# A fused attention and two-layer network kernel: halves of a tile for partial sums, and a fixed start-up order on VectorE

## The chip, the cores and the metric

The kernel runs on one core of one Trainium2 chip. The metric is the device time of one execution in microseconds (us), the median of several runs. The core's engines work side by side, each through its own list of instructions in order: TensorE (PE in the profile, with its weight loads as PEld), VectorE (DVE), ScalarE (ACT), GpSimd (POOL) and SyncE (SP). All large transfers between DRAM and the core's memory (SBUF) are issued by SP. PSUM is the memory into which TensorE writes its sums.

## The reference

Eight batches, eight heads, 576 positions, 64 values per head, 32 memories; 4608 tokens of 512 values.

```python
a = softmax(phi, axis=2)                        # over the 576 positions
k_m, v_m = a^T k, a^T v                         # 32 memories per head
attn = softmax(q k_m^T / 8)                     # over the memories
x = attn v_m                                    # -> [4608, 512]
h = x @ moe_w_in                                # 512 -> 2048
x = (h - tanh(h)) @ moe_w_out                   # 2048 -> 512
h = max(x @ w1, x @ w2, x @ w3)                 # 512 -> 768
out = h @ w_out2                                # 768 -> 512
```

The weights come as 64-bit floats, `q`, `k`, `v` and `phi` as 32-bit floats.

## The kernel before

**Numbers.** Each factor of the large products is split into a high and a low part, and `mm3` (line 115) makes three matmuls of each product: high by high, high by low, low by high. `conv` (line 160) turns a block of 64-bit weights (`raw`, three buffers) into such parts: two steps on ACT (`cvb`, `cva`), three on DVE (`cvb`), one on POOL (`cva`), and for W_out a cast on ACT and a subtraction on POOL (`wo`).

**Attention.** `phi_gen` takes the maximum of `phi` over the positions (DVE, four steps, `mx`), spreads it over the partitions by PE (`ps_mx`), and takes the exponential; `kv_mm` makes the memories (`ps_kv`, then transposed in `ps_t` to `kT`, `vT`). Per half batch, `q_front` transposes `qt` to `qT` on DVE, `q_score` makes the scores (`sc`), and `q_half` transposes them (`s`), subtracts the maximum, takes the exponential (ACT), sums rows and inverts (`st`, DVE), multiplies (POOL), transposes (`aT`, DVE) and splits into `at` (ACT and POOL). `ps_mx`, `ps_kv`, `ps_t`, `sc` and `ps_w` share two PSUM banks in turn.

**The network.** V and W_in are multiplied first: `vw_gen` makes V W_in for one batch and one quarter of W_in (`ps_w`), ACT casts it and DVE subtracts the cast (`vw`, high and low). A step takes one tile of tokens and one block `fc` of 128 features: `emit_h` makes `ps_h` from `vw` and `at` (two banks), `emit_g` makes tanh (ACT, `th`), `h - tanh(h)` (DVE, `th`), its cast (ACT) and remainder (POOL) in `gh`, and `emit_x` adds twelve matmuls, three for each of four banks `ps_x`, over the feature blocks of a tile. `emit_g` runs three steps ahead of `emit_x` and `emit_h` four.

**Order of the steps.** The features come in two phases of eight blocks. In phase 0 the first four tiles, of 288 tokens each (batches 0 and 1), take blocks 0 to 3 one tile after another (steps 0 to 15), and then blocks 4 to 7 (steps 16 to 31). After that come, for each pair of batches, tiles of 320, 512 and 320 tokens with all eight blocks; the 512-wide tile has 256 tokens of either batch. The sums of a tile at its last block go from `ps_x` to `xo` (DVE and ACT copy them in turn) and to DRAM (`xd`, line 627). Before block 4 the first four tiles load their sums back into `xo` (line 613), and at block 7 DVE adds them (line 620) and they are stored again. `xo` has one buffer.

**What sets the order on the engines.** The code is written as generators, stepped by `slot` between the products. A scheduler then sets the order on each engine, after a timeline that it estimates itself. Ties are added by hand: while `background` is set, an instruction called through V, S, T or G stands behind the `mark` of its engine (`behind`, line 64), without a wait. SP issues its transfers in order. The start (lines 662 to 691) writes out the first instructions by hand: W_in (`w0`) is converted beside `kv_mm(0)`, then come `q_gen(0, 0)`, `vw_gen(0, 0, 0)`, five steps of W_out (`wo0`), and `q_gen(0, 1)` beside six more of W_out.

Of the kernel before, what the change touches and what calls it, by code (L numbers as in the profile page):

```python
# [7 lines left out]
F32 = mybir.dt.float32  # L8
# [3 lines left out]
ALU = mybir.AluOpType  # L12
# [10 lines left out]
def kernel(  # L23
# [43 lines left out]
    background = [False]  # L67
    V, S, T, G = (Paced(e) for e in (nc.vector, nc.scalar, nc.tensor, nc.gpsimd))
    DMA = nc.sync
# [62 lines left out]
            tc.add_manual_dep(b, a.name, mybir.DependencyInfo(mybir.DependencyClass.NoSync, mybir.DependencyReason.DATA), reason="side by side")  # L132


    live = [0]

    def fetch(src):
        live[0] += 1
# [9 lines left out]
    def convs(*jobs, ahead=2):  # L148
        raws, k = [], 0
        for src, hi, lo in jobs:  # L150
            if k == len(raws):
                raws.append(fetch(src))
                yield
            while len(raws) < len(jobs) and live[0] < ahead:
                raws.append(fetch(jobs[len(raws)][0]))
            k += 1
            yield
            yield from conv(raws[k - 1], hi, lo)

    def conv(raw, hi, lo=None):  # L160
        a = cv_p.tile([P, 512], U32, tag="cva", bufs=2, name="cva")
        b = cv_p.tile([P, 512], U32, tag="cvb", bufs=2, name="cvb")
        hw, lw = raw[:, :, 1], raw[:, :, 0]
        S.activation(f(b), f(hw), AF.Abs)
        S.activation(a, lw, AF.Copy, scale=2.0 ** -29)
        yield
        V.tensor_scalar(f(b), f(b), TINY, HUGE, ALU.max, ALU.min)
        V.tensor_scalar(b, b, 3, 0x3FFFFFF8, ALU.logical_shift_left, ALU.bitwise_and)
        yield
        V.scalar_tensor_tensor(out=b, in0=hw, scalar=0xC0000000, in1=b, op0=ALU.bitwise_and, op1=ALU.bitwise_or)  # L170
        live[0] -= 1
        yield
        if lo is None:
            G.tensor_add(hi.bitcast(U32), b, a)
            yield
            return
        G.tensor_add(a, b, a)
        x = f(a).rearrange("p (k c) -> p k c", k=hi.shape[1]) if len(hi.shape) == 3 else f(a)
        S.copy(hi, x)
        yield  # L180
        G.tensor_sub(lo, x, f(hi))
        yield
# [134 lines left out]
    def q_half(b, hf):  # L317
        at = at_t[0, b]
        o = slice(hf * NH, (hf + 1) * NH)
        sp = place(b, 1 if hf else 2, [P, 2, NH], "s")  # L320
        s = sp.rearrange("p e (j m) -> p e j m", m=M)
        scs = scs_t[hf]
        for e in range(2):
            freed[e] = V.transpose(out=sp[:, e], in_=scs[e]).ins
        yield
        st = ap.tile([P, 2, JH, 3], F32, tag="st", bufs=2, name="st")
        V.reduce_max(st[:, :, :, 0], s, axis=AX.X)
        V.tensor_tensor(out=s, in0=s, in1=st[:, :, :, 0:1].to_broadcast([P, 2, JH, M]), op=ALU.subtract)
        yield
        S.activation(sp, sp, AF.Exp, scale=0.125)  # L330
        yield
        V.reduce_sum(st[:, :, :, 1], s, axis=AX.X)
        V.tensor_scalar(st[:, :, :, 2], st[:, :, :, 1], 1e-9, None, ALU.add)
        V.reciprocal(st[:, :, :, 2], st[:, :, :, 2])
        yield
        G.tensor_tensor(out=s, in0=s, in1=st[:, :, :, 2:3].to_broadcast([P, 2, JH, M]), op=ALU.mult)
        yield
        aT = place(b, 0 if hf else 3, [P, 2, NH], "aT")
        V.transpose(out=aT, in_=sp)
        yield  # L340
        at_cast.append(S.copy(at[:, 0, :, o], aT).ins)
        G.tensor_sub(at[:, 1, :, o], aT, f(at[:, 0, :, o]))
        yield
        DMA.dma_start(out=at_d[b][:, :, :, o], in_=f(at[:, :, :, o]))
        yield
# [14 lines left out]
    def q_gen(b, hf):  # L360
        if hf == 0:
            yield from q_begin(b)
        yield from q_front(b, hf)
        yield from q_score(b, hf)
        yield from q_half(b, hf)
        if hf:
            yield from q_next(b)
# [42 lines left out]
    def upto(g, word):  # L410
        for w in g:
            yield
            if w == word:
                return
# [4 lines left out]
    def vw_gen(ph, b, fq):  # L419
        while 2 * ph + fq not in wi:  # L420
            bg.need("wi2")
        t = at_p.tile([P, 2, 2, FQ], F32R, tag="vw", bufs=4, name="vw")
        pss = [bank(e, [P, FQ], "ps_w") for e in range(2)]
        small([(pss[e][32 * r:32 * r + 32], vT[b][64 * e:64 * e + 64, r], wi[2 * ph + fq][64 * e:64 * e + 64, r])
               for r in reversed(range(HP)) for e in range(2)])
        yield
        for e in range(2):
            S.copy(t[:, e, 0], pss[e])
            yield
            freed[e] = V.tensor_sub(t[:, e, 1], pss[e], f(t[:, e, 0])).ins  # L430
            yield
        vw_t[ph, b, fq] = t
# [162 lines left out]
    def at_load(b):  # L595
        at = at_t[1, b] = at_p.tile([P, 2, 2, NS], F32R, tag="at", bufs=3, name="at")
        DMA.dma_start(out=f(at), in_=at_d[b])
        yield

    def emit_x(i):  # L600
        ph, (t0, nt, pcs), fc, first, final = steps[i]
        while 8 * ph + fc not in wo_t:
            bg.need("wo")
        wt = wo_t[8 * ph + fc]
        gh = g_t.pop(i)
        if first:
            emit_x.ps = [ps_x.tile([P, NT], F32, tag=f"x{dm}", bufs=1, name=f"ps_x{dm}")[:, :nt] for dm in range(KD)]
        o = slice(t0, t0 + nt)
        add = ph or t0 < NXI and fc >= 4
        if fc == 4 and add or final and not add:  # L610
            emit_x.xo = ga_p.tile([P, KD, NT], F32, tag="xo", bufs=1, name="xo")[:, :, :nt]
            if add:
                DMA.dma_start(out=emit_x.xo, in_=xd[0][:, :, o])
        for dm in range(KD):
            T.mark = mm3(emit_x.ps[dm], (wt[:, 0, dm * P:(dm + 1) * P], wt[:, 1, dm * P:(dm + 1) * P]),
                (gh[:, 0], gh[:, 1]), first, final)
            if final:
                ps, xo = emit_x.ps[dm], emit_x.xo
                if add:
                    V.tensor_add(xo[:, dm], ps, xo[:, dm])  # L620
                else:
                    (S.copy if dm % 2 else V.tensor_copy)(xo[:, dm], ps)
            if dm == 0 and i + LG < len(steps):
                emit_g(i + LG)
            slot()
        if final:
            DMA.dma_start(out=xd[ph][:, :, o], in_=emit_x.xo)
# [16 lines left out]
    def drain(*gens):  # L644
        gens = list(gens)
        while gens:
            for g in list(gens):
                try:
                    next(g)
                except StopIteration:  # L650
                    gens.remove(g)
# [16 lines left out]
    drain(load_q(0, 1))  # L668
    next(w0)
    drain(phi_gen(0))  # L670
    drain(kv_mm(0), w0)
    wo0 = wo_conv(range(4), wo_p)
    next(wo0)
    next(wo0)
    load_phi(1, fetch.last)
    load_kv(1, fetch.last)
    drain(q_gen(0, 0))
    drain(vw_gen(0, 0, 0))
    for _ in range(5):
        next(wo0)  # L680
    S.mark = at_cast[-1]
    background[0] = True
    drain(q_gen(0, 1), part_of(wo0, 6))
    background[0] = False
    bg.add("wo", wo0)
# [312 lines left out]
```

## Time and profile before

| | |
|---|---|
| time, median of 3 runs | 1346.94 us (1345.87 to 1349.36) |
| the profiled execution's own time | 1347.29 us |
| its span in the profile | 1345.4 us |
| mean granted TensorE clock | 0.989 |
| PE busy (matmuls) | 1273.1 us, 95% |
| PEld busy (weight loads) | 1152.7 us, 86% |
| DVE, ACT, POOL busy | 748.3, 508.0, 530.2 us: 56%, 38%, 39% |
| DMA | 264.94 MB, 197 GB/s on average |

The span runs from the first to the last instruction of the profiled execution; its own time is 1.9 us longer. Busy shares are averages over the whole span. In the rows further below, "PE ps_x L57 <- DVE xo L57" reads: PE, about to write `ps_x`, waited for DVE's work on `xo`. All operations that go through the helper carry its line 57, so tiles tell them apart; DMAs carry their own lines.

### The profile page before, as it was taken

What the parts mean: (1) busy time and instruction counts of PE and PEld (TensorE: products, weight loads), DVE (VectorE), ACT (ScalarE), POOL (GpSimd) and SP (SyncE); (2) the same over time, 40 slices, a digit from 0 to 9 for tenths busy, and PEclk for the clock granted to TensorE, in tenths of its full rate; (3) what the DMA queues carried; (4) which work ended last, traced back from release to release, by engine and by line L of the source; (5) the groups of instructions that cost most, each with busy time, mean ns of one, the idle gap of its engine ahead of it and who ended that gap; (6) DMA issues with size and microseconds to landing.
All of it is one profiled execution on the core that took longest, in us unless ns stands there. A gap on an engine that the chain in (4) does not pass through costs nothing.

```text
span 1345.4 us, 22714 instructions
## 1 busy us (share of the span) xinstructions
PE 1273.1 (95%) x8996; PEld 1152.7 (86%) x8996; DVE 748.3 (56%) x1189; ACT 508.0 (38%) x993; POOL 530.2 (39%) x470
## 2 busy tenths in 40 slices
PE   3579789999999999999999999999999999999998
PEld 1467668888799798998989899899899899999996
DVE  3887648766454665757543335545645556457342
ACT  2445235454344454645553322322322323123221
POOL 1646325654344556766663431232311313123110
PEclk9989889999999999999999999999999999999999
DMA  8886678768162545766672158847557376475532
GB/s 203 233 223 187 151 188 219 226 189 235 36 248 66 182 145 202 279 232 221 235 245 97 52 219 343 321 141 287 175 215 283 106 296 243 124 298 188 176 122 47
DMA packets 188394, 264.94 MB, mean 197 GB/s; under 512 B 94976, under 2 KB 160512, under 8 KB 179200
## 3 DMA queue, kind: packets, MB, share of 16 engines
q1 hardware_dynamic: 188000, 259.82, 59.2%
q0 software_dynamic: 288, 3.67, 0.7%
q8 instruction: 71, 1.16, 0.4%
q14 instruction: 35, 0.29, 0.1%
HBM read 199.49 MB, written 63.96 MB: 196 GB/s over the span
## 4 chain that ended last, share of the span: by engine, by line
PE 84%; DVE 6%; SPq 3%; DMA 3%; issue 2%; POOL 1%; ACT 1%; DVEq 0%; POOLq 0%; ACTq 0%
PE b L57 41%; PE ps_x L57 26%; PE ps_h L57 13%; SPq L224 3%; DVE cvb L57 2%; PE ps_w L57 2%; PE ps_kv L57 1%; DMA raw<-in_moe_w_out_dram 1%; DVE th L57 1%; DMA xo<-xd 1%; DVE st L57 1%; DMA phi<-in_phi_dram 1%; ACT cvb L57 1%; DVE s L57 0%; PE sc L57 0%
## 5 line engine op out<-in xcount | busy, mean ns | idle before, releaser
L57 PE MATMUL ps_x<-gh,wo 128*128 128x320 f32 (+2 forms) x2400 | 453.7, 337 | 17.5 <-DVE xo L57 13.7
L57 PEld LDWEIGHTS ps_x<-gh,wo 128*128 128x128 f32 x2400 | 383.2, 192 | 62.3 <-issue 22.9
L57 PE MATMUL b<-mv,sw 128*128 128x384 f32 x2268 | 401.4, 338 | 0.0
L57 PEld LDWEIGHTS b<-mv,sw 128*128 128x128 f32 x2268 | 399.1, 188 | 1.2
L57 POOL TENSOR_TENSOR gh<-th,gh 128x320 fp32r<-128x320 f32 (+2 forms) x200 | 207.5, 1039 | 250.8 <-ACT gh L57 237.6
L57 PE MATMUL ps_h<-at,vw 128*128 128x256 f32 (+2 forms) x1536 | 247.9, 301 | 13.2 <-DVE th L57 6.7
L57 PEld LDWEIGHTS ps_h<-at,vw 128*128 128x128 f32 x1536 | 221.9, 191 | 37.8 <-DVE th L57 12.5
L57 DVE TENSOR_TENSOR th<-ps_h,th 128x320 f32<-128x320 f32 (+2 forms) x200 | 106.9, 535 | 180.0 <-ACT th L57 179.3
L57 ACT ACTIVATE th<-ps_h 128x320 f32<-128x320 f32 (+2 forms) x200 | 95.4, 477 | 176.2 <-PE ps_h L57 162.3
L57 PE MATMUL b<-wz,mh 128*128 128x512 f32 x648 | 150.4, 390 | 1.1 <-DVE ob L57 1.1
L57 PEld LDWEIGHTS b<-wz,mh 128*128 128x128 f32 x648 | 121.3, 188 | 26.4 <-DVE ob L57 2.0
L57 ACT CAST gh<-th 128x320 fp32r<-128x320 f32 (+2 forms) x200 | 99.9, 499 | 108.4 <-DVE th L57 90.9
L57 POOL TENSOR_TENSOR c<-c,u 128x384 f32<-128x384 f32 x36 | 36.5, 1013 | 226.2 <-ACT u L57 226.2
L57 ACT COPY p<-b 128x384 f32<-128x384 f32 x108 | 51.7, 479 | 169.5 <-PE b L57 147.0
L57 DVE TENSOR_TENSOR c<-b,u 128x384 f32<-128x384 f32 x72 | 39.8, 553 | 97.4 <-PE b L57 97.4
L57 DVE TENSOR_SCALAR cvb<-cvb 128x512 f32<-128x512 f32 x112 | 67.3, 601 | 32.3 <-ACT cvb L57 29.9
L57 DVE TENSOR_TENSOR m<-c,m 128x768 f32<-128x768 f32 x72 | 69.0, 958 | 5.0
L57 DVE TENSOR_TENSOR c<-b,p 128x384 f32<-128x384 f32 x72 | 37.7, 554 | 37.9 <-ACT p L57 34.4
L57 DVE TENSOR_TENSOR vw<-ps_w,vw 128x512 fp32r<-128x512 f32 x64 | 41.3, 682 | 28.1 <-ACT vw L57 28.1
L57 POOL TENSOR_TENSOR mv<-xr,mv 128x384 fp32r<-128x384 f32 x30 | 48.9, 1663 | 12.4 <-PE b L57 9.3
L57 POOL TENSOR_TENSOR m<-m,u 128x384 f32<-128x384 f32 x18 | 21.4, 1188 | 81.6 <-ACT u L57 80.2
L57 ACT CAST mh<-m 128x384 fp32r<-128x384 f32 (+1 forms) x54 | 31.8, 620 | 57.1 <-DVE m L57 57.1
(82 smaller groups left out, 1048.5 us busy)
## 6 DMA issues: line engine op xcount, KB each, us to landing
sw<-sw_d SPq DMA_DIRECT2D x52, 1792.0 KB, 7.5
sw_d<-so SPq DMA_DIRECT2D x9, 1792.0 KB, 7.5
raw<-in_moe_w_out_dram SPq DMA_DIRECT2D x22, 512.0 KB, 5.4
qt<-in_q_dram SPq DMA_DIRECT2D x128, 72.0 KB, 3.3
at_d<-at SPq DMA_DIRECT2D x16, 576.0 KB, 5.3
at<-at_d SPq DMA_DIRECT2D x8, 1152.0 KB, 5.7
raw<-in_moe_w_dram SPq DMA_DIRECT2D x18, 512.0 KB, 4.0
out_dram<-ob SPq DMA_DIRECT2D x144, 64.0 KB, 1.7
```

Of the source, the lines that this page charges most:

```text
L57: i = op(*a, **kw)
L224: q_dma.dma_start(out=t[64 * e + 32 * h:64 * e + 32 * h + 32, r], in_=src[e, h, r])
```

## The change

Two things. First, `xo` becomes a pair of halves for the first four tiles: one tile `two`, 576 columns wide, made once, of which tiles 0 and 2 use the left half and 1 and 3 the right (`part_x`). Loads of partial sums into it are written in `emit_x` two steps ahead of a tile's block 4, not in it. Second, the start is written out anew: `V.mark` is set to the second transpose of the scores, then to the last step of the last W_in block, then to the reciprocal of the row sums, then to the last subtraction of V W_in, so that on DVE scores, last W_in block, row sums, V W_in and W_out follow in that order.

```diff
-    live = [0]
+    live, wi_last, st_last = [0], [None], [None]
@@ convs
+            if k == len(jobs):
+                yield "last"
             yield from conv(raws[k - 1], hi, lo)
@@ conv
-        V.scalar_tensor_tensor(out=b, in0=hw, scalar=0xC0000000, ...)
+        wi_last[0] = V.scalar_tensor_tensor(out=b, in0=hw, scalar=0xC0000000, ...).ins
@@ q_half
-        V.reciprocal(st[:, :, :, 2], st[:, :, :, 2])
+        st_last[0] = V.reciprocal(st[:, :, :, 2], st[:, :, :, 2]).ins
@@
+    def part_x(t0):
+        k = t0 // NH % 2
+        return emit_x.two[:, :, k * NH:(k + 1) * NH]
+
@@ emit_x
-        add = ph or t0 < NXI and fc >= 4
-        if fc == 4 and add or final and not add:
-            emit_x.xo = ga_p.tile([P, KD, NT], F32, tag="xo", bufs=1, name="xo")[:, :, :nt]
+        parted = ph == 0 and t0 < NXI
+        add = ph or parted and fc >= 4
+        if i == 0:
+            emit_x.two = ga_p.tile([P, KD, 2 * NH], F32, tag="xo", bufs=1, name="xo")
+        if parted:
+            emit_x.xo = part_x(t0)
+        elif fc == 4 and add or final and not add:
+            emit_x.xo = ga_p.tile([P, KD, 2 * NH], F32, tag="xo", bufs=1, name="xo")[:, :, :nt]
             if add:
                 DMA.dma_start(out=emit_x.xo, in_=xd[0][:, :, o])
+        ph1, (t1, n1, _), fc1, _, _ = steps[min(i + 2, len(steps) - 1)]
+        if ph1 == 0 and t1 < NXI and fc1 == 4:
+            DMA.dma_start(out=part_x(t1), in_=xd[0][:, :, t1:t1 + n1])
@@ the start
-    drain(kv_mm(0), w0)
+    drain(kv_mm(0), upto(w0, "last"))
     wo0 = wo_conv(range(4), wo_p)
     next(wo0)
     next(wo0)
     load_phi(1, fetch.last)
     load_kv(1, fetch.last)
-    drain(q_gen(0, 0))
-    drain(vw_gen(0, 0, 0))
+    drain(q_begin(0), q_front(0, 0))
+    drain(q_score(0, 0))
+    x = q_half(0, 0)
+    next(x)
+    V.mark = freed[1]
+    background[0] = True
+    drain(w0)
+    V.mark = wi_last[0]
+    next(x)
+    next(x)
+    background[0] = False
+    y = vw_gen(0, 0, 0)
+    next(y)
+    next(x)
+    V.mark = st_last[0]
+    background[0] = True
+    drain(x, y)
+    V.mark = freed[1]
     for _ in range(5):
         next(wo0)
     S.mark = at_cast[-1]
-    background[0] = True
     drain(q_gen(0, 1), part_of(wo0, 6))
     background[0] = False
```

The first place is SP's list from the store of tile 2's first sums on. `xd_120` holds the partial sums in DRAM; `phi`, `kv` and `qt` are loads for the next batches. Before:

```order
L627 DMA xd_120<-xo 512x1x288
L198 DMA phi<-in_phi_dram 128x8x128
L199 DMA phi<-in_phi_dram 64x8x32
L211 DMA kv<-in_k_dram 128x8x256
L214 DMA kv<-in_k_dram 64x8x64
L211 DMA kv<-in_v_dram 128x8x256
L214 DMA kv<-in_v_dram 64x8x64
L224 DMA qt<-in_q_dram 32x18x32 x8
L627 DMA xd_120<-xo 512x1x288
L224 DMA qt<-in_q_dram 32x18x32 x7
L613 DMA xo<-xd_120 128x4x288
L224 DMA qt<-in_q_dram 32x18x32
```

After:

```order
L641 DMA xd_120<-xo 512x1x288
L627 DMA xo<-xd_120 128x4x288
L200 DMA phi<-in_phi_dram 128x8x128
L201 DMA phi<-in_phi_dram 64x8x32
L213 DMA kv<-in_k_dram 128x8x256
L216 DMA kv<-in_k_dram 64x8x64
L213 DMA kv<-in_v_dram 128x8x256
L216 DMA kv<-in_v_dram 64x8x64
L226 DMA qt<-in_q_dram 32x18x32 x8
L641 DMA xd_120<-xo 512x1x288
L226 DMA qt<-in_q_dram 32x18x32 x8
L627 DMA xo<-xd_120 128x4x288
```

The load of tile 0's sums moved from behind the second group of `qt` loads to right behind tile 2's store; the load of tile 1's sums (the last row of after) keeps its place behind sixteen `qt` loads.

The second place is DVE's list in the start. `cvb` is a block of weights, and takes two `TENSOR_SCALAR` and one `SCALAR_TENSOR_TENSOR`: in the rows of before the first such block is the last one of W_in, the second the first one of W_out. Before:

```order
L57 TENSOR_SCALAR cvb<-cvb 128x512 x2
L57 SCALAR_TENSOR_TENSOR cvb<-raw,cvb 128x512
L57 STREAM_TRANSPOSE qT<-qt 128x576
L57 TENSOR_SCALAR cvb<-cvb 128x512
L57 STREAM_TRANSPOSE s<-sc 128x288 x2
L57 TENSOR_SCALAR cvb<-cvb 128x512
L57 TENSOR_REDUCE st<-s 128x18
L57 SCALAR_TENSOR_TENSOR cvb<-raw,cvb 128x512
L57 TENSOR_TENSOR s<-s,st 128x576
L57 TENSOR_TENSOR vw<-ps_w,vw 128x512
L57 TENSOR_REDUCE st<-s 128x18
L57 TENSOR_SCALAR st<-st 128x18
```

After:

```order
L57 STREAM_TRANSPOSE s<-sc 128x288 x2
L57 TENSOR_SCALAR cvb<-cvb 128x512 x2
L57 SCALAR_TENSOR_TENSOR cvb<-raw,cvb 128x512
L57 TENSOR_REDUCE st<-s 128x18
L57 TENSOR_TENSOR s<-s,st 128x576
L57 TENSOR_REDUCE st<-s 128x18
L57 TENSOR_SCALAR st<-st 128x18
L57 RECIPROCAL st<-st 128x18
L57 TENSOR_TENSOR vw<-ps_w,vw 128x512
L57 STREAM_TRANSPOSE aT<-s 128x576
L57 TENSOR_TENSOR vw<-ps_w,vw 128x512
L57 TENSOR_SCALAR cvb<-cvb 128x512
```

The last W_in block now stands behind the transposes of the scores and ahead of the maximum, the row sums stand ahead of both subtractions `vw`, and the first W_out block begins behind these.

The third place is the entry of batch 3 (`vT_92` holds its V) at the first 512-wide tile, on PE. `wo_962` to `wo_964` are the W_out parts of the last three blocks of the 320-wide tile before it; the four numbers behind `ps_x` are its four banks, and `ps_x_2756` is a bank of the 512-wide tile. Before:

```order
L57 MATMUL ps_x_2495<-gh,wo_962 128x320 x3
L57 MATMUL ps_x_2496<-gh,wo_962 128x320 x3
L57 MATMUL ps_w<-wi,vT_92 32x512 x8
L57 MATMUL ps_x_2497<-gh,wo_962 128x320 x3
L57 MATMUL ps_x_2498<-gh,wo_962 128x320 x3
L57 MATMUL ps_h<-at,vw 128x256 x6
L57 MATMUL ps_x_2495<-gh,wo_963 128x320 x3
L57 MATMUL ps_x_2496<-gh,wo_963 128x320 x3
L57 MATMUL ps_h<-at,vw 128x256 x2
L57 MATMUL ps_x_2497<-gh,wo_963 128x320 x3
L57 MATMUL ps_x_2498<-gh,wo_963 128x320
L57 MATMUL ps_h<-at,vw 128x256 x3
```

After:

```order
L57 MATMUL ps_x_2491<-gh,wo_964 128x320 x3
L57 MATMUL ps_t<-ident,n 64x128 x4
L57 MATMUL ps_w<-wi,vT_92 32x512 x8
L57 MATMUL ps_h<-at,vw 128x256 x10
L57 MATMUL ps_w<-wi,vT_92 32x512 x8
L57 MATMUL ps_h<-at,vw 128x256 x2
L57 MATMUL sc<-qT,kT 32x288 x8
L57 MATMUL ps_h<-at,vw 128x256 x12
L57 MATMUL ps_x_2756<-gh,wo_296 128x512
```

On DVE, at the same place, after:

```order
L57 TENSOR_TENSOR n<-ps_kv,rc 128x2x2x64
L57 TENSOR_TENSOR mx<-phi 128x256
L57 COPY xo<-ps_x_2488 128x320
L57 TENSOR_TENSOR mx<-mx,phi 128x256
L57 COPY xo<-ps_x_2490 128x320
L57 TENSOR_TENSOR mx<-mx,phi 128x256 x2
L57 TENSOR_TENSOR vw<-ps_w,vw 128x512 x4
L57 TENSOR_TENSOR th<-ps_h,th 128x512
```

V W_in of batch 3 moved on PE from among the products of the old tile to behind the last of them, and on DVE the four `vw` stand behind the four `mx`, which are batch 5's maximum; before, DVE had the four `vw` (two pieces, with `cvb` between) right ahead of the first 512-wide `th`, and the `mx` further ahead.

## Rows read from the trace of the kernel before

**Rows 1.** Windows: busy us of each engine (instructions), granted clock, DMA share, GB/s.

```profile
core 0: us, PE busy (x) PEld busy (x) DVE busy (x) ACT busy (x) POOL busy (x), PEclk, DMA share, GB/s
0.00:1345.40 1345.40, 1273.13 (x8996) 1152.72 (x8996) 748.26 (x1189) 507.97 (x993) 530.18 (x470) 0.99 0.60 197
145.00:150.00 5.00, 0.64 (x16) 0.10 (x16) 0.00 (x0) 1.30 (x2) 0.00 (x0) 1.00 0.79 123
185.00:190.00 5.00, 0.43 (x2) 0.43 (x3) 0.94 (x3) 0.00 (x0) 0.00 (x0) 0.50 0.82 175
200.00:250.00 50.00, 50.00 (x512) 42.20 (x511) 39.49 (x67) 26.91 (x50) 27.94 (x25) 1.00 0.72 196
```

**Rows 2.** Waits from 100 to 215 us: us in total, times, longest us.

```profile
DVE xo L57 <- DMA xo<-xd: 15.4, 3, 7.2
PE ps_x L57 <- DVE xo L57: 13.7, 2, 7.0
```

**Rows 3.** Timeline of SP: start us, us, operation, count.

```profile
114.34 0.52 SPq L627 DMA_DIRECT2D xd<-xo  x1
...
131.02 10.27 SPq L224 DMA_DIRECT2D qt<-in_q_dram  x8
141.39 0.57 SPq L627 DMA_DIRECT2D xd<-xo  x1
142.06 5.09 SPq L224 DMA_DIRECT2D qt<-in_q_dram  x7
147.20 0.63 SPq L613 DMA_DIRECT2D xo<-xd  x1
...
184.69 0.58 SPq L613 DMA_DIRECT2D xo<-xd  x1
```

**Rows 4.** Timeline of PE around its two waits for `xo`.

```profile
138.92 1.75 PE L57 MATMUL ps_x<-gh,wo 128*128 128x288 f32 x12
...
152.66 6.17 PE L57 MATMUL ps_x<-gh,wo 128*128 128x288 f32 x28 [7.01 <-DVE xo L57]
...
162.54 2.92 PE L57 MATMUL ps_x<-gh,wo 128*128 128x288 f32 x20
...
189.57 8.87 PE L57 MATMUL ps_x<-gh,wo 128*128 128x288 f32 x46 [6.70 <-DVE xo L57]
```

**Rows 5.** Timeline of the start, by engine.

```profile
41.97 1.26 POOL L57 TENSOR_TENSOR wo<-cva,wo 128x512 fp32r<-128x512 f32 x1 [0.73 <-ACT wo L57]
...
42.06 1.20 DVE L57 TENSOR_SCALAR st<-st 128x18 f32<-128x18 f32 x1
...
47.88 2.77 PE L57 MATMUL ps_h<-at,vw 128*128 128x288 f32 x10 [0.64 <-POOL at L57]
...
69.13 1.43 DVE L57 STREAM_TRANSPOSE qT<-qt 128x576 f32<-128x576 f32 x2
...
87.65 0.18 DVE L57 TENSOR_SCALAR st<-st 128x18 f32<-128x18 f32 x1
```

**Rows 6.** Waits of DVE from 28 to 50 us.

```profile
DVE cvb L57 <- ACT cvb L57: 3.7, 3, 2.2
DVE aT L57 <- POOL s L57: 0.7, 1, 0.7
DVE vw L57 <- ACT vw L57: 0.6, 1, 0.6
```

**Rows 7.** DMA issues from 120 to 155 us: KB each, median us to landing.

```profile
phi<-in_phi_dram SPq DMA_DIRECT2D x1, 512.0 KB, 4.4
```

**Rows 8.** Timeline from 206 to 229 us, around batch 3's first V W_in.

```profile
206.47 0.84 SPq L198 DMA_DIRECT2D phi<-in_phi_dram  x1
...
213.41 0.42 DVE L57 TENSOR_TENSOR mx<-phi 128x256 f32<-128x256 f32 x1 [1.23 <-DMA phi<-in_phi_dram]
...
213.93 3.11 DVE L57 TENSOR_TENSOR mx<-mx,phi 128x256 f32<-128x256 f32 x3
...
216.97 1.09 PE L57 MATMUL ps_w<-wi,vT 64*32 64x512 f32 x16
...
220.10 1.06 ACT L57 CAST vw<-ps_w 128x512 fp32r<-128x512 f32 x2
...
220.71 1.29 DVE L57 TENSOR_TENSOR vw<-ps_w,vw 128x512 fp32r<-128x512 f32 x2 [1.01 <-ACT vw L57]
```

More of the change, by code (lines that the diff above doesn't have):

```diff
@@ L169, in conv @@
         yield
-        V.scalar_tensor_tensor(out=b, in0=hw, scalar=0xC0000000, in1=b, op0=ALU.bitwise_and, op1=ALU.bitwise_or)
+        wi_last[0] = V.scalar_tensor_tensor(out=b, in0=hw, scalar=0xC0000000, in1=b, op0=ALU.bitwise_and, op1=ALU.bitwise_or).ins
         live[0] -= 1
```

## The prediction

> **What bounds the kernel now.** I read the stretches first, then TensorE's waits, then the queue that serves the longest wait. TensorE (PE) is busy for 1273.1 of 1345.4 us, so only its idle time and its slow time can be won. In 200 to 250 us it is busy throughout; ahead of that, two stretches stand out: PE does 0.64 of 5 us in 145 to 150 and 0.43 of 5 us in 185 to 190, where the granted clock is 0.50, the lower of its two levels (1.2 instead of 2.4 GHz) [rows 1]. One wait makes both: PE wants a `ps_x` bank, and VectorE (DVE) has not emptied it, 13.7 us in two waits; DVE itself stands before the same additions for 15.4 us in three, because `xo` has not been loaded [rows 2].
>
> The queue says why [rows 3]. The sums of the first four tiles' first half wait in DRAM and come back through one tile `xo`. The store of tile 2 left at 114.34, and no load could go until tile 3's sums had been copied into the same `xo` and stored. That store (141.39) stands behind eight `qt` loads (131.02, 10.27 us), the first load behind seven more (142.06, 5.09 us). It left at 147.20; the twelve products whose sums it was for had ended at 140.67 [rows 4]. Tile 2's load has the same fate: it waits for tile 1's sums to be loaded, added and stored behind another batch's loads, and left at 184.69. DVE runs in order, so while it waits nothing else of its work goes on either: 0.00 us busy in 145 to 150 [rows 1].
>
> **The change, part by part.** *The two halves.* Tiles 0 and 2 use one half, 1 and 3 the other, and a load is written two steps ahead. In the new order tile 0's load stands right behind tile 2's store, that is at about 115 instead of 147, some 26 us ahead of its use. Tiles 2 and 3 get their loads right behind the stores of tiles 0 and 1. The number of transfers and of additions stays. So both waits go: **-13.7 us**. With them goes the slow clock behind each: 28 products took 6.17 us and 46 took 8.87, while 20 of the same shape took 2.92 at full clock, 0.146 each [rows 4]. 28 x (0.220 - 0.146) + 46 x (0.193 - 0.146) = **-4.2 us**.
>
> *Tile 1's load* stays behind the sixteen `qt` loads, at about 147.9 on the old clock, and lands some 5 us later (issued at 147.20 [rows 3], the wait over at 152.66 [rows 4], less an addition), so at about 152.7. Without the first wait PE reaches the end of tile 1 early: from 140.7 (the end of tile 0's last step) 48 products of `ps_x`, 24 of `ps_h` and some small ones, 74 x 0.146 = 10.8 us, to 151.5, and then 16 score products and six more `ps_h`, 1.5 us by estimate, before the bank is wanted. That is a tie: **+1 us**, bounds 0 (a quicker landing) and 4 (a landing as late as the second wait is long, less the lead).
>
> *DVE's order up to the first tile.* It removes and adds nothing but order; the same W_out pieces come before the first `th`. DVE's avoidable waits in 28 to 50 are 0.7 for `aT`, 0.6 for `vw`, and 3.7 - 2.2 = 1.5 for `cvb` (the 2.2 is the load of the last W_in block, which stays) [rows 6]. To these comes a stretched instruction: `st` took 1.20 at 42.06 and 0.18 at 87.65 [rows 5], 1.0 us. So at most 3.8 us. What stays on the path: scores, maximum, exponential, sum, GpSimd's product, transpose, `at`, each on the engine before. The ten `ps_h` products that started at 47.88 [rows 5] move ahead by at most that, but the first `ps_x` also needs W_out, which now comes wholly behind V W_in, and GpSimd has four W_out pieces ahead of the first `gh`. I take **-2 us**, the middle of 0 and -4.
>
> The `st` of 1.20 us began while GpSimd was in a W_out piece (41.97, 1.26 us [rows 5]). The Trainium skill, SBUF — State Buffer, section "SBUF: two separate sides", says that VectorE and GpSimd share a port pair as an exclusive lock: whichever starts first keeps it for its whole instruction. By that rule the W_out pieces, now close together, would stretch each other again and the start-up gain would be near 0; the sum would be 2 us higher. The row agrees with it, one time.
>
> *What is late next.* The scheduler places later work anew, and one place tells. Batch 3 enters at the first 512-wide tile. Its V W_in needs PSUM banks that `ps_kv` and `ps_t` of batch 4 hold first. Before, it stood 42 `ps_x` products ahead of that tile's first step; now it stands behind the last product of the tile before, and on DVE its low parts (`vw`) stand behind all four `mx` of batch 5. These wait for a load of `phi` which only the end of batch 4's `ps_kv` lets go. The nearest case of before: `phi` issued at 206.47, the first `mx` at 213.41 after a wait for it, the last one over at 217.04, 10.6 us in all [rows 8]. A quicker landing of `phi` is 4.4 us [rows 7]; with four `mx` of 0.42 and two copies, taken as long, that makes 6.9. PE needs 4.4 us from that issue to the end of the old tile (24 products of 320 columns at 0.146 x 320/288 = 0.162, and a few short ones, 0.5 in all at the 0.07 of a `ps_w` product [rows 8]). So `vw` starts V = 2.5 to 6.2 us after PE has run dry. From there: two subtractions 1.29, the second V W_in product (sixteen matmuls) 1.09, two casts 1.06 [rows 8], the rest of the subtractions 0.65, scores and six `ps_h` 1.5, tanh and cast about 0.6 each = V + 6.8 until `ps_x` can go on, while PE's own work there is `ps_t`, two V W_in, scores and 24 `ps_h`, 6.5 us by estimate. So PE loses V + 0.3 = 2.8 to 6.5, middle 4.7, plus up to 2 us for a lowered clock (the two waits above cost 2.1 each at 7 us idle). I take **+5.5 us**, bounds 0 (the placing does no harm) and 9. The steps' lead gives no cover here, since PE has by then used up its three steps.
>
> *The rest.* From 205 us on PE has few waits, and all DMA and attention work that follows is released by PE or DVE, so it moves ahead with them: 0, bounds -1 and +2. The tile `xo` is 576 instead of 512 columns wide: nothing waits for its size.
>
> Sum: 1347.3 (the profiled execution; its span is 1345.4, the 1.9 around it stays) - 13.7 - 4.2 + 1 - 2 + 5.5 = 1333.9. The profiled execution lies 0.35 above the median of the runs, so **1333.5 us**, 1.0% less.
>
> **The rivals.** *Nothing is handed back:* batch 3's V W_in is ready in time because `phi` lands quickly and PE's lead holds; for it, that PE is busy in all 50 us of 200 to 250 now [rows 1], so leads do hold; against it, the order. 1346.9 - 13.7 - 4.2 - 2 + 0.5 = 1327.5. *More is handed back:* tile 1's load comes 4 us late and the entry of batch 3 costs 9; for it, that the queue is pressed just there: eight `qt` loads took 10.27 us at 131.02, against 5.09 for the seven after [rows 3]. 1346.9 - 17.9 + 4 + 9 - 1 = 1341. *The halves do not part:* if the wait were on the whole tile, load 2 would still wait for tile 1's store and both waits would stay: 1345 with the start-up's gain; in the new order the load stands ahead of that store, which speaks against it. *Slower than before:* the queue at the start. The fourth W_out load waits for a `raw` buffer which DVE frees with the first W_out block, now behind V W_in, and thirteen `qt` loads of batch 1 stand behind it. They take 0.7 each (5.09 for seven [rows 3]), 9 us; their use is at 69.13 and they could leave from about the first `ps_h`, 47.88 [rows 5], which with 5 us of landing leaves some 7 us of slack. Each us beyond it delays batch 1 and all behind it; from some 20 us of waiting on, the 13.4 us are gone and the kernel is slower, 1349 at 23. Nothing in the trace makes a W_out block that late.
>
> **How the numbers follow.** Forecast (part is handed back, 1329 to 1338) 0.60; nothing handed back 0.16; more handed back (1338 to 1344) 0.15; halves don't part 0.04; slower by the queue 0.05. The range reaches from the middle of the second to past the middle of the third: 1327 to 1342. Differences under 0.3%, 4 us, cannot be told from none here: faster by more is the first three cases less the late end of the third, 0.87; same 0.08; slower 0.05.
>
> **What would show it.** Right: no wait of PE on DVE's `xo` over 2 us, full clock in 140 to 185, the first load of `xo` at about 115; PE idle in several pieces of 1 to 2 us ahead of the first 512-wide `ps_x`, with DVE waiting for `phi`. Wrong: a wait of DVE's `xo` on the load of tile 1 over 4 us; the first `ps_h` not earlier than 47; batch 1's `qT` waiting for `qt`; a new wait later than 205 us that gives away more than 9 us.

## The result, and the profile after

The changed kernel is slower: 1353.42 us, median of 7 runs (1350.09 to 1362.58), against 1346.94 for the kernel before (7 runs, 1343.29 to 1349.36). The ratio is 1.0072, with a 95% interval from 1.0049 to 1.0096. I had forecast 1.0% less. The profiled execution took 1350.09 us, with a span of 1348.2; it is the fastest of the seven, and its mean granted clock is the highest, 0.989 against 0.978 to 0.986 in the others.

Windows of the profile after, the columns as in [rows 1]:

```profile
0.00:1348.20 1348.20, 1274.54 (x8996) 1153.32 (x8996) 747.37 (x1189) 506.95 (x993) 534.11 (x470) 0.99 0.60 197
50.00:70.00 20.00, 13.35 (x67) 12.88 (x67) 16.77 (x26) 8.95 (x20) 16.85 (x13) 0.74 0.60 143
145.00:150.00 5.00, 5.00 (x40) 5.00 (x39) 3.51 (x11) 2.16 (x6) 2.39 (x3) 1.00 0.90 202
185.00:190.00 5.00, 5.00 (x35) 5.00 (x36) 4.43 (x8) 2.25 (x5) 2.15 (x3) 1.00 1.00 283
200.00:260.00 60.00, 53.26 (x613) 41.74 (x614) 38.88 (x66) 23.63 (x44) 27.63 (x23) 0.91 0.72 202
240.00:250.00 10.00, 8.21 (x166) 5.81 (x165) 7.50 (x11) 4.48 (x8) 9.29 (x8) 0.62 0.33 114
```

The two holes of [rows 1] are full: PE works through 145 to 150 and 185 to 190 at full clock. A new hole lies in 200 to 260, where PE is idle for 6.7 us and the granted clock falls to 0.62 in 240 to 250; and the start runs at 0.74 in 50 to 70, where the kernel before had 0.91:

```profile
50.00:70.00 20.00, 15.34 (x92) 12.89 (x92) 19.21 (x30) 9.10 (x19) 15.01 (x12) 0.91 0.68 185
```

The waits for `xo` from 100 to 215 us, which were 15.4 and 13.7 in [rows 2]:

```profile
DVE xo L57 <- DMA xo<-xd: 2.5, 1, 2.5
...
PE ps_x L57 <- DVE xo L57: 0.3, 1, 0.3
```

And the queue that fed them, SP's timeline (compare [rows 3]):

```profile
119.09 0.53 SPq L641 DMA_DIRECT2D xd<-xo  x1
122.38 0.59 SPq L627 DMA_DIRECT2D xo<-xd  x1
...
135.01 8.81 SPq L226 DMA_DIRECT2D qt<-in_q_dram  x8
143.93 0.57 SPq L641 DMA_DIRECT2D xd<-xo  x1
144.60 5.80 SPq L226 DMA_DIRECT2D qt<-in_q_dram  x8
150.44 0.63 SPq L627 DMA_DIRECT2D xo<-xd  x1
```

The first load now leaves at 122.38, behind the store of tile 2; tile 1's load, behind the sixteen `qt` loads, costs the one wait that is left.

So the holes are gone, and the time went elsewhere. Where it went is read from the steps: a step ends with its twelfth `ps_x` product, so every twelfth of PE's 2400 such products gives the end of one. The table holds them for the profiled executions, as differences from the kernel before (negative is ahead). The kernels of the experiments stand beside it for later.

| end of step | before, us | changed | halves alone | start alone, no further step | further step alone | halves, V W_in first, W_out late |
|---|---|---|---|---|---|---|
| 0 | 54.69 | +3.57 | +0.32 | -0.22 | -0.09 | +1.24 |
| 19 | 140.66 | +4.23 | -0.19 | +6.80 | -0.78 | +0.69 |
| 32 | 208.36 | -19.66 | -21.28 | +2.67 | -4.62 | -20.82 |
| 39 | 231.03 | -19.58 | -21.21 | +2.39 | -4.83 | -20.88 |
| 40 | 235.48 | -8.43 | -11.13 | +2.39 | -4.84 | -14.66 |
| 43 | 249.41 | +3.22 | -3.98 | +2.39 | -4.84 | -14.41 |
| 48 | 274.49 | +1.02 | -6.22 | +2.39 | -4.00 | -14.00 |
| 103 | 475.41 | -0.34 | -6.18 | +3.60 | -2.54 | -12.26 |
| 152 | 641.29 | +2.49 | -6.18 | +3.60 | +0.28 | -12.26 |
| 199 | 792.62 | +2.49 | -6.18 | +3.60 | +0.27 | -12.26 |

The changed kernel begins some 4 us late, is 19.6 us ahead at step 39, and has lost it all by step 43. Two cautions. The kernel with the further step alone has the order of before on every engine up to 218 us and was still 4.62 us ahead at step 32: two executions of one order differ by that much. And being ahead by steps is not all gain, since small products (`ps_kv`, `ps_w`, `sc`) may have moved behind the step: the last column loses 6.5 us between steps 39 and 43 while PE is hardly idle. So a second table gives PE's idle time (span less busy time) by stretches, from the windows; a slow clock shows in it as longer busy time.

| PE idle, us | before | changed | halves alone | start alone, no further step | further step alone | halves, V W_in first, W_out late |
|---|---|---|---|---|---|---|
| 0 to 140 | 48.9 | 51.7 | 48.3 | 50.7 | 49.5 | 49.0 |
| 140 to 200 | 13.8 | 2.3 | 3.4 | 10.4 | 11.2 | 3.0 |
| 200 to 260 | 0.0 | 6.7 | 5.3 | 0.0 | 0.0 | 0.2 |
| 260 to 400 | 0.9 | 1.8 | 0.4 | 0.0 | 1.6 | 0.6 |
| 400 to the end | 8.7 | 11.2 | 8.6 | 8.6 | 11.0 | 8.7 |
| idle in all | 72.3 | 73.7 | 65.9 | 69.7 | 73.3 | 61.5 |
| busy in all | 1273.1 | 1274.5 | 1273.2 | 1279.4 | 1272.5 | 1271.9 |

Against before, the changed kernel wins 11.5 us of idle time in 140 to 200 and loses 2.8 ahead of it, 7.6 in 200 to 400, and 2.5 behind.

The entry of batch 3, step 40, on PE and DVE (timeline, profile after):

```profile
207.76 3.69 PE L57 MATMUL ps_x<-gh,wo 128*128 128x320 f32 x24
...
211.38 0.66 PE L57 MATMUL ps_t<-ident,n 128*64 128x128 f32 x8
...
211.59 0.43 DVE L57 TENSOR_TENSOR mx<-phi 128x256 f32<-128x256 f32 x1 [1.70 <-DMA phi<-in_phi_dram]
...
212.57 1.09 PE L57 MATMUL ps_w<-wi,vT 64*32 64x512 f32 x16 [0.53 <-ACT vT L57]
...
214.37 1.29 DVE L57 TENSOR_TENSOR vw<-ps_w,vw 128x512 fp32r<-128x512 f32 x2 [0.36 <-ACT vw L57]
...
219.16 0.72 PE L57 MATMUL sc<-qT,kT 64*32 64x288 f32 x16 [1.62 <-DVE vw L57]
...
221.34 0.62 PE L57 MATMUL ps_x<-gh,wo 128*128 128x512 f32 x2
```

Behind it, steps 41 to 43, on SP, ACT and PE:

```profile
217.02 7.62 SPq L226 DMA_DIRECT2D qt<-in_q_dram  x8
...
225.42 5.98 SPq L226 DMA_DIRECT2D qt<-in_q_dram  x8
...
230.93 2.22 PE L57 MATMUL ps_x<-gh,wo 128*128 128x512 f32 x8
...
232.11 3.04 SPq L141 DMA_DIRECT2D raw<-in_moe_w_out_dram  x2
...
237.53 0.66 ACT L57 ACTIVATE cvb<-raw 128x512 f32<-128x512 f32 x1 [6.53 <-DMA raw<-in_moe_w_out_dram]
...
239.35 1.63 POOL L57 TENSOR_TENSOR gh<-th,gh 128x512 fp32r<-128x512 f32 x1 [7.49 <-ACT gh L57]
...
242.14 0.71 PE L57 MATMUL ps_kv<-ones,phi 128*32 128x1 f32 x40 [1.79 <-issue]
...
248.42 4.21 PE L57 MATMUL ps_x<-gh,wo 128*128 128x512 f32 x9
```

The first fence is the forecast term: `ps_x` stands from 211.4 to 221.3 while V W_in is made and split; the load of `phi` (1.70) plays a smaller part in it than the turns between PE, ACT and DVE. The second fence was in no term. ACT stood for 6.53 us before the load of a W_out block, which SP could issue only at 232.11 behind sixteen `qt` loads; casts and tanh were queued behind it (`gh` on POOL waited 7.49), and after the idle pieces nine products took 4.21 us at 248.42, 0.47 each, where eight of that width had taken 2.22 at 230.93, 0.28 each.

### The profile page after: what moved, and what is told of

Read it like the earlier page. It is cut to its first block, busy times and chain, and to the rows that moved or that the text cites. A ratio compares the mean times of both kernels' runs of the same rounds, so it can differ in the third digit from the quotient of the medians.

```text
span 1348.2 us, 22719 instructions
## 1 busy us (share of the span) xinstructions
PE 1274.5 (95%) x8996; PEld 1153.3 (86%) x8996; DVE 747.4 (55%) x1189; ACT 506.9 (38%) x993; POOL 534.1 (40%) x470
## 4 chain that ended last, share of the span: by engine, by line
PE 81%; DVE 6%; DMA 6%; SPq 3%; issue 2%; ACT 2%; POOL 1%; DVEq 0%; ACTq 0%; POOLq 0%
PE b L57 40%; PE ps_x L57 24%; PE ps_h L57 12%; DVE cvb L57 2%; DMA raw<-in_moe_w_out_dram 2%; PE ps_w L57 2%; PE ps_kv L57 2%; SPq L226 2%; DMA phi<-in_phi_dram 1%; DMA kv<-in_v_dram 1%; DMA sw<-sw_d 1%; DVE th L57 1%; DVE st L57 1%; ACT cvb L57 1%; PE sc L57 1%
## 5 line engine op out<-in xcount | busy, mean ns | idle before, releaser
L57 ACT COPY p<-b 128x384 f32<-128x384 f32 x108 | 51.7, 479 | 170.2 <-PE b L57 141.9
L57 POOL TENSOR_TENSOR mv<-xr,mv 128x384 fp32r<-128x384 f32 x30 | 48.9, 1662 | 12.4 <-ACT mv L57 12.4
```

The costliest lines, as they stand in the source:

```text
L57: i = op(*a, **kw)
```

## The experiments

All ratios are against the kernel before on the same chip, whose median lay between 1344.2 and 1346.0 us there. "The further step" is a third part of the change that I found only on the way; it comes with experiment 9. The step times in some of the expectations are off: counted product by product, as in the table, the changed kernel's first step ends 3.6 us late and the sixteenth 4.2, the waits that are gone give 23.8, and steps 40 to 43 take 22.8 back, 11.2 of it at step 40; the halves alone give back 17.2 of 21.2, 10.1 of it at step 40.

**1 and 2: the halves alone, the start alone.** The first is the kernel before with `part_x`, `two` and the early loads (and none of the rest); the second is the changed kernel with `emit_x` of before.

> The two halves alone, with the start as before. In the trace of the changed kernel the first step ends 2.9 us later than before, the sixteenth 4; the two waits for xo then give 21, and steps 40 to 43 (the first 512-wide tile) take 19 of it back. Theory 1, the chain of batches (scores, V W_in and the next batch's memories take turns in two PSUM banks, and this chain did not move when the waits went): the chain starts 4 us earlier than in the changed kernel, so all that follows does: 1346 to 1349, about the time before, and the loss of the changed kernel is its start. Rival, the start costs nothing in the end, since slack behind it takes it up: 1350 to 1354, like the changed kernel.

> The fixed order of VectorE at the start alone, xo as before. Theory 1: the 3 to 4 us of the start stay to the end, since nothing behind it has slack while the two waits for xo remain: 1350 to 1352. Rival, the waits for xo take the late start up (they wait for a queue, not for the start): 1346 to 1348.

Measured: halves 1341.53 us, ratio 0.998 (0.9967 to 0.9994); start 1355.40 us, 1.0087 (1.0068 to 1.0106). Neither number is what theory 1 gave: the halves are 0.2% faster, and the start with all else of the change costs more than the whole loss. The halves alone are at 1341 in microseconds, the time of my second rival, but the kernel before was at 1344.24 beside them; on the forecast's 1346.9 their ratio gives 1344.

**3 and 4: the two places of the hand-back, each cured alone in the changed kernel.** Experiment 3 issues V W_in of batch 3 before the memories of batch 4; experiment 4 begins the second half of W_out later.

```diff
# 3, in q_beside, for b == 3: the memories of the next batch last
+        if b == 3:
+            for g in (x, y, x, y, x, y, x):
+                yield next(g, None)
+            yield from y
+            yield "half"
+            yield from m
+            return
# and ("q", 0, 3) is queued behind ("vw", 0, 3, fq)
# 4
-        bg.add("wos", wo_store(fc), start[0, 2])
+        bg.add("wos", wo_store(fc), start[0, 2] + 24)
```

> The changed kernel, with V W_in of batch 3 issued ahead of the memories of batch 4 and not behind them; nothing else is changed, and the work is the same. In its order both V W_in of batch 3 stand at steps 38 and 39.5 and not behind step 40. Theory 1: step 40 loses its wait, some 9 of the 19 us are kept, 1341 to 1345 by the profiled execution of the changed kernel (1350). Rival 1, the chain is only shifted: batch 4's memories come later by the same, and its first tile (step 56) or the slow clock takes the time back, 1349 to 1354. Rival 2, the loss lies in the W_out conversions at steps 41 to 43 alone: step 40 stays as long, no gain, 1350 to 1354.

> The changed kernel, with the conversion of the second half of W_out begun 24 steps later (step 56 and not 32), so that ScalarE does not wait for its weights (6.5 us in one wait, with tanh and cast queued behind it) in steps 40 to 43. Theory of that wait: the 9.6 us that steps 41 to 43 hand back are kept, 1341 to 1345, and step 40 still loses 9. Theory 1: what ScalarE gains there is not on the chain of batches, and the time comes back by step 56: 1347 to 1353.

Measured: V W_in first 1352.43 us, 1.0068 (1.0046 to 1.0091), no gain on the changed kernel; W_out late 1344.08 us, 0.9997 (0.998 to 1.0013), 0.7% better than it. In experiment 3 rival 1 holds, though not at step 56: it loses 6.2 us at step 40 where the changed kernel loses 11.2, is 9.3 us ahead of before at the end of step 43, and 1.7 at the end of step 64, the first step of the 512-wide tile that batch 5 enters. The wait was moved to the next such tile. Experiment 4 gives 9 us by the medians (5.4 by the profiled executions), and where the wait on ACT was priced: over steps 41 to 43 it loses 4.4 us against before, the changed kernel 11.7.

**5 and 6: one turn less in the chain.** A batch's `ps_kv`, `ps_t`, two `ps_w`, two `sc` and `ps_mx` take turns in the two small banks. Both kernels leave out the maximum of `phi` for batches 2 to 7, in the halves and in the kernel before.

```diff
+        if b >= 2:
+            S.activation(ph, ph, AF.Exp)
+            yield
+            ph_t[b] = ph
+            yield
+            return
         mx = ap.tile([P, H, M], F32, tag="mx", bufs=1, name="mx")
```

> The two halves alone (start as before), and for batches 2 to 7 the maximum of phi is neither taken nor subtracted: that leaves out one of the seven turns that a batch takes in the two small PSUM banks (two products on TensorE of 1.1 us per batch, 6.8 in all, and some 4.5 us per batch on VectorE). In its order V W_in of batch 3 stands at steps 30 and 32 and not at 40. To be read against the same cut in the kernel before. Theory 1, the chain of turns took the gain back: without one turn the gain of the halves stays, 15 to 20 us below the kernel before with the same cut: about 1319. Rival, the gain is lost elsewhere: 2 to 6 us below it, about 1333.

> The kernel before with the same cut as in the run above: no maximum of phi for batches 2 to 7. The two waits for xo stay, as they hang on the queue and not on the chain. TensorE loses 6.8 us of products: 1337 by both theories; if it falls by much more (under 1330), the chain bounded the kernel before as well.

Measured: halves 1333.55 us, 0.9907 (0.9889 to 0.9925); before 1342.18 us, 0.9967 (0.9954 to 0.9981). So with the cut the halves are worth 0.6%, 8.6 us, and without it 0.2%. That is three times as much and half of what theory 1 said. The kernel before gains 3.4 us by the cut, half of the 6.8 of the products left out. One reason is in the waits of the cut kernel before, whose holes are smaller (13.7 in [rows 2]):

```profile
PE ps_x L57 <- DVE xo L57: 8.7, 2, 5.2
```

And of that gain nothing is lost at the entry: the cut halves are 6.1 us ahead of the cut kernel before at the end of step 39 and at that of step 43, and PE has no idle time there, against 5.3 us in the halves without the cut (windows of 200 to 260 us, first with, then without the cut):

```profile
200.00:260.00 60.00, 60.00 (x554) 50.04 (x553) 35.72 (x63) 30.26 (x57) 34.61 (x29) 1.00 0.64 187
```

```profile
200.00:260.00 60.00, 54.73 (x649) 42.57 (x649) 43.13 (x74) 26.40 (x50) 30.55 (x26) 1.00 0.76 211
```

Batch 4's `ps_kv` starts at 167.1 us in the cut halves and at 201.7 in the halves. The cut takes out a turn in the banks and DVE's steps for the maximum at once, so which of the two the chain hung on is not shown.

**7 and 8: which tie of the start, and W_out late in the halves.** Experiment 7 takes from the changed kernel the tie that holds W_out behind V W_in; experiment 8 is experiment 4's edit on the halves.

```diff
# 7
     drain(x, y)
-    V.mark = freed[1]
+    V.mark = None
+    background[0] = False
     for _ in range(5):
         next(wo0)
     S.mark = at_cast[-1]
+    background[0] = True
```

> The changed kernel without one of its four ties: W_out's conversion on VectorE is no longer held behind V W_in (its first block stands among the scores again); scores, last W_in block, row sums and V W_in stay tied. Theory S, holding back W_out is what the start costs (ScalarE then stands 3.1 us before the load of the third W_out block, and the first products of ps_x wait for W_out): 1341 to 1344, like the two halves alone. Rival, the order among scores, W_in and V W_in costs it: 1349 to 1354.

> The two halves alone, with the conversion of the second half of W_out begun at step 56 and not 32. The halves alone gave back 8 of 19 us at steps 40 to 43, 6 at step 40 and 2 behind it. Theory of the wait on ScalarE (5.5 us there too): the 2 behind step 40 are kept, and what the queue is relieved of: 1337 to 1340. Rival, in the changed kernel the late start was what made that wait cost time, here it costs nothing: 1341 to 1343.

Measured: W_out free 1354.12 us, 1.0046 (1.0026 to 1.0067); halves with W_out late 1342.17 us, 0.9968 (0.9953 to 0.9984), no clear gain on the halves. Experiment 7 did not fit theory S, and its steps said why: it was 18.2 us ahead at step 39, and 8.3 behind at step 199. The start could not be what it lost between these. Something of the change acts all along the program.

**9 to 12: the further step.** `convs` now yields "last" before the last block of every call, though only the first W_in conversion has a reader for it. The conversions are paced by counting steps, so each block of W_out's second half takes nine and not eight, and all later work is placed anew.

```diff
# 9 and 11: the halves, and the kernel before, with this alone
             k += 1
             yield
+            if k == len(jobs):
+                yield "last"
             yield from conv(raws[k - 1], hi, lo)
# 10 and 12: the changed kernel, and the start alone, without it elsewhere
-            if k == len(jobs):
+            if tell and k == len(jobs):
                 yield "last"
# tell is set by wi_conv(0) alone
```

> The two halves with the start as before, and one more thing of the change that the runs so far kept apart from neither: convs hands out the word last ahead of the last block of every job, which is one step more for every paced conversion of weights (9 steps and not 8 for each block of the second half of W_out, of w1 to w3's and of w_out2's). Theory Y, this step, and not the start, costs the time, since it puts the conversions at other places all along the program: 1349 to 1354. Rival S, the order of the start costs it: 1340 to 1343, like the halves alone.

> The changed kernel, with the word last handed out for the first W_in conversion alone, where the start needs it; halves and start order as changed. Theory Y: 1340 to 1346 (the halves alone, plus the 2 to 4 us by which the first steps end later). Rival S: 1350 to 1354, as changed.

> The kernel before with nothing but the further step in every conversion. Theory Y: slower, 1350 to 1356, with the two waits of 1 us each for xo at 500 to 700 us that all kernels with this step showed. Rival S: 1343 to 1347, as before.

> The order of the start alone (xo as before), without the further step in the other conversions. Theory Y: 1344 to 1349, as before or up to 4 us later, the lateness of the first steps. Rival S: 1352 to 1357, like the start with that step.

Measured, with experiments 1 and 2 and the changed kernel as the other corners:

| ratio to before | no further step | further step |
|---|---|---|
| as before | 1 | 1.0039 (1.0024 to 1.0053) |
| halves | 0.998 (0.9967 to 0.9994) | 1.0019 (1.0007 to 1.003) |
| start order | 1.0056 (1.0044 to 1.0069) | 1.0087 (1.0068 to 1.0106) |
| both | 1.0037 (1.0023 to 1.0051) | 1.0072 (1.0049 to 1.0096) |

In us, experiments 9 to 12 measured 1348.22, 1348.80, 1348.76 and 1351.69, beside 1344.64 for the kernel before: each lies between the ranges of its two theories. Both were half right, and the three parts add up: along every edge of the table the halves give 0.15 to 0.2%, the start costs 0.48 to 0.57%, the step costs 0.31 to 0.39%, each difference uncertain by 0.2 to 0.3%. In us: -2.5, +7 and +5.

The step's cost has at least one place in the trace. The kernels with it show, in the waits of PE from 480 to 720 us, what the kernel before, the halves and experiments 10 and 12 do not have (experiment 11; the idle table has it in its row from 400 us on):

```profile
PE ps_x L57 <- DVE xo L57: 2.3, 2, 1.3
```

These two waits lie between the ends of steps 103 and 152. There every kernel with the step (the changed one and experiments 2, 3, 4, 7, 9 and 11) takes 2.8 us longer than before, and every kernel without it as long as before. That is somewhat more than half of the step's cost.

The start's cost is read from experiment 12, which has nothing else. Its waits of PE from 40 to 72 us hold one that is not there before, and its clock is 0.75 in 50 to 70:

```profile
PE ps_mx L57 <- DVE mx L57: 5.0, 1, 5.0
```

`mx` is the maximum of batch 1's `phi`, queued on DVE behind the W_out blocks. It is no later than before; PE comes to it earlier, behind 32 products of `ps_x` and not 40 (timelines, first before, then experiment 12):

```profile
60.21 0.74 DVE L57 TENSOR_TENSOR mx<-phi 128x256 f32<-128x256 f32 x1
...
64.41 0.63 PE L57 MATMUL ps_mx<-ident,mx 128*128 128x128 f32 x2
```

```profile
58.02 0.75 DVE L57 TENSOR_TENSOR mx<-phi 128x256 f32<-128x256 f32 x1
...
62.64 0.66 PE L57 MATMUL ps_mx<-ident,mx 128*128 128x128 f32 x2 [4.99 <-DVE mx L57]
```

By step 19 the kernel is 6.8 us late. Up to there PE makes the same 1041 matmuls in both (windows to the end of step 19, first before, then experiment 12):

```profile
0.00:140.66 140.66, 91.76 (x1041) 72.66 (x1041) 99.95 (x170) 58.83 (x120) 64.75 (x64) 0.95 0.79 206
```

```profile
0.00:147.46 147.46, 96.80 (x1041) 77.17 (x1041) 101.38 (x170) 59.20 (x120) 66.38 (x64) 0.90 0.75 202
```

So 5.0 of the 6.8 us are longer matmuls at a lower clock, and 1.8 are idle time. Over the whole span the products take 6.3 us more than before (1279.4 against 1273.1 busy). The clock in 50 to 70 goes with the start's order: it is 0.74 to 0.76 in the six kernels that have all of it (changed, 2, 3, 4, 10, 12), 0.91 or 1.00 in the nine with the start of before, and 1.00 and 0.83 in experiments 7 and 15, which leave out the tie on W_out.

**13 to 15: both places at once, and the start's tie again.** Experiment 13 is experiment 3's edit on the halves, 14 adds experiment 4's, 15 is experiment 7 without the further step.

> The two halves alone, start as before and without the further step, with V W_in of batch 3 ahead of the memories of batch 4. In the changed kernel the same edit kept 6 us at step 40 and lost them at step 64. Theory 1 (the chain of turns, which this edit does not shorten): moved, not cured: 1340 to 1344, as the halves alone. Rival, what moved it there was the start and the further step: the gain of step 40 stays, 1334 to 1338.

> The run above with the conversions of the second half of W_out begun at step 56. Theory 1: no more than the halves with that edit alone, 1340 to 1343. Rival: both gains add up, 1332 to 1337.

> The changed kernel without the further step in the other conversions and without the tie that holds W_out behind V W_in; scores, last W_in block, row sums and V W_in stay tied. If the tie on W_out is the start's whole cost: 1341 to 1343 (the halves alone). If it is half of it, as the run with the further step said (0.26%): 1344 to 1347. If it is none: 1348 to 1350.

Measured: 13, 1343.07 us, 0.9973 (0.996 to 0.9985), not told apart from the halves; 14, 1335.66 us, 0.9921 (0.9902 to 0.994), where the rival holds; 15, 1346.68 us, 0.9999 (0.9983 to 1.0016). Experiment 14 is what the halves were meant to be: faster than both kernels, by 0.8% and 1.5%. Each of its two edits alone gives the halves some 0.1%, less than the intervals, both together 0.6%. In its windows PE is idle for 0.2 us where the halves had 5.3:

```profile
200.00:260.00 60.00, 59.83 (x684) 48.06 (x683) 35.89 (x67) 23.42 (x45) 24.72 (x21) 1.00 0.60 158
```

Experiment 15 against 10 (1.0037) puts some 0.4% on the tie that holds back W_out (experiment 7 against the changed kernel: 0.26%, within the intervals), 3.5 to 5 of the start's 7 us. The size is loose: the medians themselves, 1346.68 and 1348.80 beside kernels before that differ by 1.4 us, are 2.1 us apart. The rest stays with the other ties, about the width of the intervals.

## Why the prediction was wrong, step by step

**The waits for `xo`** (-13.7 and -4.2) were right in cause and too large. In the halves they fall from 13.7 us to 1.3 (the `ps_x` wait on `xo`), but PE's idle time in 140 to 200 falls by 10.4 only, since other short waits come up where the long ones had covered them. The 4.2 us of slow clock are not found in the sum: the clock rose from 0.86 to 0.97 in 140 to 200, and yet PE is busy for 1273.2 us in all, as before. Here the terms' size failed, by 3.3 and 4.2 us.

**Tile 1's load** (+1, a tie): right. DVE waited 2.5 us for it, PE 0.3.

**The start** (-2, bounds 0 and -4) failed, and in sign. The ten `ps_h` products did move ahead by 2.5 us (47.88 in [rows 5]), as DVE's avoidable waits said; but the step had already named what made that worthless, that the first `ps_x` needs W_out, "which now comes wholly behind V W_in", and then took the middle of a range that ended at 0. What was behind W_out on DVE was not asked at all: the first `th` and `mx`. Timeline of the profile after:

```profile
45.36 2.67 PE L57 MATMUL ps_h<-at,vw 128*128 128x288 f32 x10
...
46.32 0.67 ACT L57 ACTIVATE cvb<-raw 128x512 f32<-128x512 f32 x1 [3.10 <-DMA raw<-in_moe_w_out_dram]
...
51.70 0.44 DVE L57 TENSOR_TENSOR th<-ps_h,th 128x288 f32<-128x288 f32 x1
...
52.20 1.81 PE L57 MATMUL ps_h<-at,vw 128*128 128x288 f32 x6 [3.55 <-DVE th L57]
...
53.81 1.16 PE L57 MATMUL ps_x<-gh,wo 128*128 128x288 f32 x4
...
60.73 0.76 DVE L57 TENSOR_TENSOR mx<-phi 128x256 f32<-128x256 f32 x1
...
65.37 0.66 PE L57 MATMUL ps_mx<-ident,mx 128*128 128x128 f32 x2 [4.46 <-DVE mx L57]
```

In the kernel before, DVE came to these two no later:

```profile
51.50 0.45 DVE L57 TENSOR_TENSOR th<-ps_h,th 128x288 f32<-128x288 f32 x1
...
60.21 0.74 DVE L57 TENSOR_TENSOR mx<-phi 128x256 f32<-128x256 f32 x1
```

ACT, whose list has the tanh behind W_out's blocks too, waits 3.10 us for the load of one. So PE, which is ready sooner, waits 3.55 us for `th`, has its first `ps_x` at 53.81 (52.90 before), and then stands 4.46 us for `mx`. The measured price is +7 us (experiments 2, 10 and 12). The waits counted were those that go; the waits that come, for DVE's work behind the moved blocks, and the slow clock beside them are what counts.

The rule cited from the Trainium skill (SBUF — State Buffer, "SBUF: two separate sides"), which the page limits to VectorE's operations in a two-port mode, or with two inputs in SBUF against a GpSimd operation that reads SBUF, fits the W_out blocks. For the `st` of [rows 5], with one input, no row shows the mode. The rows of after agree, one with GpSimd idle and one beside it, both with two inputs:

```profile
47.37 0.69 DVE L57 SCALAR_TENSOR_TENSOR cvb<-raw,cvb 128x512 uint32<-128x512 uint32 x1
...
48.20 1.31 POOL L57 TENSOR_TENSOR cva<-cvb,cva 128x512 uint32<-128x512 uint32 x1 [3.49 <-DVE cvb L57]
...
48.42 1.63 DVE L57 SCALAR_TENSOR_TENSOR cvb<-raw,cvb 128x512 uint32<-128x512 uint32 x1
```

But it is not what the start costs: up to step 19 DVE's same 170 instructions take 101.38 us in experiment 12 and 99.95 before (windows above).

**What is late next** (+5.5, bounds 0 and 9) named the right place. The wait is there, though less for `phi` than for the turns between PE, ACT and DVE. In the halves alone it has its size too: 5.3 us of idle time in 200 to 260. In the changed kernel it was too small, 6.7 idle and a clock of 0.91 there: the sum followed V W_in to the first `ps_x` of the tile and took everything behind it to be ready, and in steps 41 to 43 ACT's wait for a load and the lowered clock came on top. Why PE runs dry there is seen from the orders: without the holes PE reaches batch 4's `ps_kv` at step 38 and not 32, while by the clock its products with `kv` start at 203.8, and in the kernel before at 203.1. From batch 3's `ps_kv` to batch 4's it is 43.7 us before and 44.4 changed. The chain of turns did not move with the products, so what they win beyond the slack of that chain is lost where PE next needs it. Which link sets the chain's pace is not shown. A shorter chain cures it (experiment 5: no idle time there), and so does other work out of its way (experiment 14: 0.2).

**The further step** had no term. I had read `yield "last"` as a signal for the start, and the part "the rest" (0, bounds -1 and +2) rested on nothing else having changed later. It cost 5 us, 2.8 of them between the ends of steps 103 and 152. With this and the start, the terms that failed make 14 us of the distance between -13.4 and +9.7 us (the forecast and 0.72% of 1346.9); the sum for the halves alone, -17.9 + 1 + 5.5 = -11.4, against -6.3 in their profiled execution and -2.5 by the medians, makes most of the rest.

**The rivals.** "More handed back", 1341, is the time of the halves alone in microseconds, but by luck of the base: by the ratio they are at 1344. The slower case had the wrong mechanism: batch 1's `qt` loads did not decide (DVE waited 0.5 us for them, as before); what stands behind W_out did. Of the signs of being wrong the last came true: a wait later than 205 us that gives away more than 9 us.

What stays open: where the further step costs the 2 us beyond the 2.8; and how the rest of the start, without the tie on W_out, divides.

## What to carry to other kernels

When a stall goes, find the second chain that ran beside it, and ask from its own times (here: when batch 4's memories start) how far the main engine can run ahead before it needs that chain; then price every queue that serves the chain in the steps behind, not only the first wait. Two causes at one place can each hide the other: cured singly in the halves they were worth some 0.1%, together 0.6%. And where background work is paced by counting the steps of generators, an added `yield` is a change to the whole schedule, to be kept where its reader is.

## What the runs showed that I had not expected

Short idle pieces can cost the clock as one long wait does, or not: in the changed kernel 6.7 us of them in 200 to 260 went with a granted clock of 0.62 in 240 to 250, while the halves, with 5.3 us in the same stretch, stayed at 1.00, and experiment 10, with 8.4, at 0.97. And two executions with the same order on every engine were 4.62 us apart at step 32, as much as several of the terms that I summed.
